# Two attention layers on one core, planned ahead: four buffers for B's divided products, new costs in the planner, a new order

## The chip, the cores and the metric

The kernel runs on one core of a Trainium2 chip. The metric is the device time of one execution in microseconds (us). Before the change the median of three runs is 492.5 us (491.84 to 493.69).

A core has engines with instruction queues of their own: PE (TensorE, matrix products into PSUM), DVE (VectorE), ACT (ScalarE), POOL (GpSimd) and SP (SyncE, which here only issues DMA transfers). Each engine works through its queue in the order in which it was written, and stops at an instruction whose semaphores have not arrived. So an instruction that is late holds up all that is queued behind it on its engine.

## The reference

The input x has 2048 tokens of 512 bfloat16 values. Two kinds of layer, A and B, are each applied twice, with the same weights both times.

```python
def _A_ref(x, wq, wk, wv, wo, beta):          # 32 heads of 16, 4 segments of 512 tokens
    ...
    for s in range(N):
        p = _softmax(qs @ ks.T * scale + mask)          # inside the segment
        a_dot = p @ vs
        a_mem = (phi(qs) @ M) / (phi(qs) @ z + 1e-6)    # memory of the earlier segments
        o = g * a_mem + (1.0 - g) * a_dot
        M = M + phi(ks).T @ vs; z = z + sum(phi(ks))
    return o @ wo

def _B_ref(x, wqkv, w_phi, wo):               # linear attention, 32 heads of 16
    q, k, v = split(x @ wqkv)
    pq, pk = q @ w_phi, k @ w_phi              # per head
    phi_q = concat(softmax(pq), softmax(-pq)); phi_k = concat(softmax(pk), softmax(-pk))
    kv = phi_k.T @ v;  z = sum(phi_k)          # over all 2048 tokens
    o = (phi_q @ kv) / (phi_q @ z + 1e-6)
    return o @ wo

x = x + _A_ref(_layernorm(x)); x = x + _B_ref(_layernorm(x))
x = x + _A_ref(_layernorm(x)); x = x + _B_ref(_layernorm(x))
```

In B, `kv` and `z` run over all tokens, so no output of B can be computed before the keys of the last tokens are done. In A, a segment needs only itself and the segments before it.

## The kernel before

The tokens lie in 16 tiles of 128; four tiles make a segment of A and a chunk of B. The program lists some 3470 operations (`Program.add`), each with the engines that may run it, a cost, what it reads and writes, and the tiles (buffers out of pools of fixed size) that it needs. Nothing of the order is written out by hand. A table `PLAN` gives each operation a priority; `sequence` turns the priorities and the dependences into one list, and `schedule` walks along it: for each engine it starts the next operation at the time when its inputs, a free buffer and the engine are there, by the costs given in `add`. The table `ON` says for some operations which of two engines takes them, and `PAIRS` says which products of queries and keys are interleaved with the next one on PE. Costs, landing times (`LANDS`, `took`, `at`) and table entries therefore decide three things: the order on every queue, the buffer each operation gets, and where PE gets filler. On the chip nobody looks at the planned times; semaphores decide.

Filler is a product of `warm` with itself into a free bank (`idle_op`, seen as L1586): where the planner sees PE idle, it puts in as many of them as fit. It keeps PE busy and computes nothing.

The parts of one run, in order: the loads and the first layer norm; A of the first layer over four segments (`a_att`, with the B keys and queries of the finished segments between); the step to the second layer, where all of B's keys must be done before the first output of B; the second A, with the first layer's B outputs of chunks 1 to 3 between; and at the end B's output for all 16 tiles.

The step around which the buffers of the change lie is `b_out`. For each tile of 128 tokens: PE multiplies `Rkv` with the exponentials of the queries (8 matmuls, names `PS<-Rkv,EQ` or `Rkv,KT`), DVE takes a reciprocal (L1488) and multiplies it on (L1489, `O<-PS,rd`), giving O, "the divided products". O is transposed, by PE (L877 `ident,O`, then a copy by ACT or DVE) or by a DMA transpose on SP's queue (L861 `OT<-O`). Then PE multiplies with `WB_o` (four matmuls), and the result is added to X. O comes from the pool `p_O`. The first PE instruction of a tile is given the buffer of O beforehand:

```python
self.pe([...Rkv products...], er + rk, [g2()], pre=[o, rd])
```

So these products wait on PE until the buffer that they will fill later is free, that is, until the transpose that read it has ended.

At the start, `setup` issues the loads on ACT's and SP's queues, ACT runs two exponentials of `beta` (L1001, L1002; the load of ACT's function table stands ahead of them), and `ln` (L1100 statistics, L1101, L1104, then L1106 on POOL, then L1115 `xn`) prepares the first tiles; their keys leave PSUM by L1181 (`KT<-PS,even`), scaled by `even` (L998).

Of the kernel before, what the change touches and what calls it, by code (L numbers as in the profile page):

```python
# [37 lines left out]
LANDS = 2.3  # L38
# [780 lines left out]
class Kernel:  # L819
# [272 lines left out]
    def ln(self, c, pris, groups=((0, 1), (2, 3)), by_pe=(), pool=None, gap=False):  # L1092

        R = self.R
# [537 lines left out]
```

## Time and profile before

| | |
|---|---|
| median of three runs | 492.5 us (491.84 to 493.69) |
| the profiled execution: its time | 492.46 us |
| its span in the profile | 490.7 us |
| instructions | 18973 |
| busy share PE, DVE, ACT, POOL | 96%, 90%, 87%, 55% |
| fillers (L1586) | 154 |

The profiled execution's own time is 1.8 us longer than its span, the part before the first and after the last instruction. A row of the time line has its start, its length, engine, source line, operation, output and inputs; a bracket at its end gives the idle time of the engine before it and what ended it. Line 799 is the helper that issues all matmuls, 855 the one that copies PSUM out, 861 and 863 the ones that issue DMA transposes and plain transfers, so there the names of the tiles tell the steps apart. A matmul's row is longer than the time until the next one starts, because matmuls overlap.

### The profile page before, as it was taken

How to read it: one execution, taken by the hardware profiler on the slowest of the kernel's cores; microseconds unless marked ns; L12 is line 12 of the kernel's file. 1: busy time of each engine (PE TensorE's matmuls, PEld its weight loads, DVE VectorE, ACT ScalarE, POOL GpSimd, SP SyncE). 2: the span in 40 equal slices, each digit the busy share in tenths (PEclk: the TensorE clock that was granted, in tenths of full speed). 3: DMA queues.
4: the chain of work that ended last, by engine and by line, in shares of the span. 5: the costliest groups of instructions: out<-in, count | busy, mean ns of one | idle time of the engine just before them, and what ended most of it. 6: DMA issues, size and time to landing. Idle time of an engine off the chain costs nothing.

```text
span 490.7 us, 18973 instructions
## 1 busy us (share of the span) xinstructions
PE 470.4 (96%) x8127; PEld 307.3 (63%) x8127; DVE 441.6 (90%) x979; ACT 425.7 (87%) x590; POOL 268.4 (55%) x536
## 2 busy tenths in 40 slices
PE   7998999999999999999999999999999999999896
PEld 6666666575657556647766666757665666575663
DVE  6998899998888999899999999999999697879785
ACT  4998999999999999783899999999999998968142
POOL 3865538656467769251256347566767364635242
PEclk9999999999999999999999999999999999999999
DMA  8965735521421221200434555352423231110234
GB/s 241 193 110 120 128 72 106 81 42 23 57 35 27 45 44 25 27 3 5 45 56 68 67 87 76 58 67 35 88 34 67 37 46 27 23 27 2 36 92 113
DMA packets 99156, 31.15 MB, mean 63 GB/s; under 512 B 90880, under 2 KB 99072, under 8 KB 99072
## 3 DMA queue, kind: packets, MB, share of 16 engines
q1 hardware_dynamic: 97824, 28.88, 35.4%
q8 instruction: 64, 1.05, 0.9%
q10 hardware_dynamic: 1248, 1.06, 0.7%
q14 instruction: 20, 0.16, 0.2%
HBM read 6.32 MB, written 2.10 MB: 17 GB/s over the span
## 4 chain that ended last, share of the span: by engine, by line
PE 47%; ACT 24%; DVE 22%; DMA 4%; issue 2%; ACTq 1%; POOL 0%; SPq 0%; DVEq 0%
PE PS L799 44%; ACT DT L1311 7%; ACT PT L1301 7%; DMA OT<-O 3%; DVE DT L1321 3%; ACT PT L1290 2%; ACT phi L1130 2%; DVE stats L1100 2%; DVE X L1364 2%; DVE PhiQ L1134 1%; PE PS L1586 1%; DVE O L1347 1%; DVE xn L1115 1%; PE PS L877 1%; DVE phi L1132 1%
## 5 line engine op out<-in xcount | busy, mean ns | idle before, releaser
L1317 POOL TENSOR_SCALAR_AFFINE_SELECT DT<-DT 64x256 bf16<-64x256 bf16 (+1 forms) x256 | 106.5, 436 | 72.2 <-ACT DT L1311 29.8
L1311 ACT ACTIVATE DT<-PS 128x1024 bf16<-128x1024 f32 x128 | 129.7, 1044 | 4.6 <-PE PS L799 3.7
L1301 ACT ACTIVATE PT<-PS 128x1024 bf16<-128x1024 f32 x128 | 128.9, 1038 | 4.7 <-PE PS L799 4.1
L1317 POOL TENSOR_SCALAR_AFFINE_SELECT DT<-PT 128x256 bf16<-128x256 bf16 x128 | 55.9, 445 | 50.0 <-PE PS L799 22.2
L799 PE MATMUL PS<-VT,DT 128*128 128x17 bf16 x1536 | 77.8, 171 | 0.8 <-POOL DT L1317 0.6
L799 PE MATMUL PS<-QT,KT 32*64 32x64 bf16 (+3 forms) x1280 | 72.6, 222 | 5.5 <-ACT DT L1311 0.9
L1398 POOL TENSOR_TENSOR Ek<-Ek,rZ 128x512 bf16<-128x512 bf16 x60 | 62.3, 1055 | 25.1 <-DVE rZ L1395 22.1
L799 PEld LDWEIGHTS PS<-VT,DT 128*128 128x128 bf16 x1536 | 70.6, 96 | 7.8 <-DVE X L1364 1.1
L799 PEld LDWEIGHTS PS<-QT,KT 32*128 32x128 bf16 (+1 forms) x1280 | 38.2, 97 | 50.5 <-ACT PT L1301 11.5
L799 PE MATMUL PS<-QT,KTo 32*64 32x64 bf16 (+3 forms) x1280 | 65.3, 216 | 0.0
L799 PEld LDWEIGHTS PS<-VT,PT 128*128 128x128 bf16 x1024 | 48.1, 96 | 8.7 <-issue 1.1
L799 PE MATMUL PS<-VT,PT 128*128 128x17 bf16 x1024 | 51.2, 171 | 0.1
L1321 DVE TENSOR_TENSOR DT<-PT,late 128x256 bf16<-128x256 bf16 x128 | 42.4, 347 | 5.5 <-PE PS L799 3.1
L1100 DVE BATCH_NORM_STATS2 stats<-X 128x6 f32<-128x512 bf16 x64 | 43.5, 685 | 1.6 <-ACT X L855 0.5
L1393 DVE TENSOR_REDUCE Zk<-Ek 128x64 f32<-128x1024 bf16 x32 | 38.5, 1203 | 4.2 <-ACT Ek L1392 4.1
L1106 POOL TENSOR_TENSOR rstd<-rstd,negh 128x2 f32<-128x2 f32 (+1 forms) x36 | 24.9, 693 | 30.5 <-DVE rstd L1104 27.1
L799 PEld LDWEIGHTS PS<-QT,KTo 32*128 32x128 bf16 (+1 forms) x1280 | 38.8, 99 | 0.1
L1392 ACT ACTIVATE Ek<-PS 128x512 bf16<-128x512 f32 x64 | 35.1, 631 | 3.1 <-PE PS L799 3.0
L799 PE MATMUL PS<-xnT,WA_q 128*128 128x128 bf16 x512 | 34.9, 219 | 0.1
L799 PE MATMUL PS<-WA_v,xnT 128*128 128x512 bf16 x128 | 34.8, 380 | 0.2
L799 PE MATMUL PS<-WA_o,OT 128*128 128x512 bf16 x128 | 32.8, 380 | 1.5 <-DMA OT<-O 0.8
L1290 ACT ACTIVATE PT<-PS 128x1024 bf16<-128x1024 f32 x32 | 33.1, 1053 | 0.4 <-PE PS L799 0.3
(146 smaller groups left out, 1009.7 us busy)
## 6 DMA issues: line engine op xcount, KB each, us to landing
EQ<-in_B_wqkv_dram SPq DMA_DIRECT2D x2, 512.0 KB, 8.2
out_dram<-X SPq DMA_DIRECT2D x8, 128.0 KB, 2.0
out_dram<-X SPq DMA_DIRECT2D x16, 64.0 KB, 2.0
X<-in_A_x_dram SPq DMA_DIRECT2D x6, 128.0 KB, 7.3
X<-in_A_x_dram SPq DMA_DIRECT2D x3, 256.0 KB, 6.6
OT<-O SPq DMA_TRANSPOSE x46, 2.5
xnT<-xn SPq DMA_TRANSPOSE x36, 2.5
WA_o<-in_A_wo_dram SPq DMA_DIRECT2D x1, 512.0 KB, 4.0
```

Source lines behind the costliest of these rows:

```text
L799: return e.matmul(o, l, r, start=st, stop=sp, tile_position=(basep(l), basep(o)))
L1100: self.dve(lambda e, t=t: e.bn_stats(self.stats[:, t, :], self.X[:, t, :]), 0.60, [R("X", t)], [R("stats", t)])
L1106: self.pool(lambda e, ve=ve, n=n: e.tensor_tensor(ve, ve, self.negh[:, 0:1].to_broadcast([128, n]), ALU.pow), 0.76, [R("rstd", t0 + i) for ...
L1130: self.act(lambda e: e.activation(shape(t2.ap), src(), ACT.Exp), 512, [res()], [t2()])
L1290: self.act(lambda e, st=st, pt=ta[y]: e.activation(pt.ap[:].rearrange("p b c -> p (b c)"), self.ps[:, st.slot[0] * 512:st.slot[0] * 512 + ...
L1301: self.act(lambda e, st=st, pt=pt: e.activation(pt.ap[:].rearrange("p b c -> p (b c)"), self.ps[:, st.slot[0] * 512:st.slot[0] * 512 + 102 ...
L1311: self.act(lambda e, st=st, dt=dt: e.activation(dt.ap[:, :, :, 64:320], self.ps[:, st.slot[0] * 512:st.slot[0] * 512 + 1024].rearrange("p ...
L1317: lambda e, c=c, src=src, base=base, p=p, block=block: e.affine_select(block(c, p), src() if src else block(c, p), [[0, 2], [0, 2], [1, 64 ...
L1321: P.add(("dve",), lambda e, early=early, block=block: e.tensor_tensor(block(320), early(), self.late[:, None, None, :].to_broadcast([128, ...
L1392: self.act(lambda e, sgn=sgn, Ek=Ek, gen=gen: e.activation(Ek.ap[:, sgn, :], self.bank(gen), ACT.Exp, scale=1.0 - 2.0 * sgn), 512, [gen()] ...
L1393: self.dve(lambda e, Ek=Ek, Zk=Zk: e.tensor_reduce(Zk.ap[:], Ek.ap[:].rearrange("p s (h j) -> p s h j", h=H), AX.X, ALU.add), 1.15, [Ek(0) ...
L1398: P.add(("dve", "pool") if late else ("pool",), lambda e, Ek=Ek, rZ=rZ, sgn=sgn: e.tensor_tensor(Ek.ap[:, sgn, :].rearrange("p (h j) -> p ...
```

## The change

The pool of O grows from two buffers to four. Five numbers of the planner change: the first landing (`LANDS`), the first key weights' transfer, the issue of a plain transfer (0.62 to 0.68), the power function on POOL (0.76 to 0.62) and the issue of four of the transposes of B's raw weights (1.28 to 1.7); and the two exponentials of `beta` may not be planned ahead of 5.1. With these the three tables were searched anew: every entry of `PLAN` may differ, `ON` moves 8 operations from DVE to ACT and 7 the other way, and `PAIRS` has 166 entries instead of 170. Nothing that is computed changes.

```diff
-LANDS = 2.3
+LANDS = 1.4
...
-    159, 165, 183, 201, 213, 243, 247, 249, 255, 267, ...
+    165, 177, 183, 195, 219, 243, 245, 249, 267, 273, ...
...
-        op = self.P.add(eng, f, 1.28 if transpose else 0.62, reads, writes, lat=1.5 if transpose else 1.3, isdma=True)
+        op = self.P.add(eng, f, (slow or 1.28) if transpose else 0.68, reads, writes, lat=1.5 if transpose else 1.3, isdma=True)
...
-        self.p_O = slots("O", 2, [128, 4, 128], BF16)
+        self.p_O = slots("O", 4, [128, 4, 128], BF16)
...
-        for k, took in (("k", (2.4, 0.4)), ("q", (1.2, 1.5)), ("v", (0.7, 1.2))):
+        for k, took in (("k", (1.9, 0.4)), ("q", (1.2, 1.5)), ("v", (0.7, 1.2))):
...
-        self.act(lambda e: e.activation(g_.ap[:, 0, :], self.beta[:], ACT.Exp, scale=-1.0), 32, [R("beta")], [g_(0)])
+        self.act(lambda e: e.activation(g_.ap[:, 0, :], self.beta[:], ACT.Exp, scale=-1.0), 32, [R("beta")], [g_(0)]).at = 5.1
...
-                self.transposed(lambda t=th[dt]: t.ap[:], lambda dt=dt, raw=raw: raw.ap[:, dt, :], [raw()], [th[dt]()], False, pre=[th[dt]])
+                self.dma(lambda t=th[dt]: t.ap[:], lambda dt=dt, raw=raw: raw.ap[:, dt, :], [raw()], [th[dt]()], transpose=True, slow=1.7 if k == "k" else 0.0)
...
-            self.pool(lambda e, ve=ve, n=n: e.tensor_tensor(ve, ve, self.negh[:, 0:1].to_broadcast([128, n]), ALU.pow), 0.76,
+            self.pool(lambda e, ve=ve, n=n: e.tensor_tensor(ve, ve, self.negh[:, 0:1].to_broadcast([128, n]), ALU.pow), 0.62,
```

Three places of the new order matter below. First, DVE at the very start. Before:

```order
10 L1100 BN_STATS stats<-X 128x6
11 L1101 BN_AGGR mv<-stats 128x2
12 L1003 TENSOR_SCALAR rd<-rd 128x32
13 L1104 TENSOR_SCALAR rstd<-mv 128x1
14 L1059 MEMSET Vt 128x32
15 L1100 BN_STATS stats<-X 128x6
16 L1101 BN_AGGR mv<-stats 128x2
17 L1115 TENSOR_SCALAR xn<-X,mv,rstd 128x512
18 L1104 TENSOR_SCALAR rstd<-mv 128x1
```

The same place after the change:

```order
9 L1115 TENSOR_SCALAR xn<-X,mv,rstd 128x512
10 L1104 TENSOR_SCALAR rstd<-mv 128x1
11 L1100 BN_STATS stats<-X 128x6
12 L1101 BN_AGGR mv<-stats 128x2
13 L1104 TENSOR_SCALAR rstd<-mv 128x1
14 L1115 TENSOR_SCALAR xn<-X,mv,rstd 128x512
15 L1003 TENSOR_SCALAR rd<-rd 128x32
16 L1004 RECIPROCAL rd<-rd 128x32
17 L1005 TENSOR_SCALAR cb<-rd 128x32
18 L1016 COPY VT<-cb 128x128 x2
19 L998 TENSOR_REDUCE even<-H 128x1
```

L1003, which reads an exponential of ACT, stood ahead of the first tile's L1104; now it stands behind the second tile's `xn`. `even` (L998), which was DVE's first instruction, now stands behind it too.

Second, SP's queue before the second segment of the first A. Before:

```order
26 L863 DMA WA_o<-in_A_wo_dram 128x4x512
27 L861 DMA_TRANSPOSE OT<-O 128x4x128
28 L863 DMA WB_v<-in_B_wqkv_dram 128x4x512
29 L861 DMA_TRANSPOSE OT<-O 128x4x128
30 L861 DMA_TRANSPOSE KT<-ktoke 128x4x128
31 L861 DMA_TRANSPOSE KTo<-ktoko 128x4x128
32 L861 DMA_TRANSPOSE KT<-ktoke 128x4x128
33 L861 DMA_TRANSPOSE xnT<-xn 128x4x128 x2
```

After:

```order
31 L863 DMA WA_o<-in_A_wo_dram 128x4x512
32 L861 DMA_TRANSPOSE OT<-O 128x4x128 x2
33 L861 DMA_TRANSPOSE KTo<-ktoko 128x4x128
34 L861 DMA_TRANSPOSE KT<-ktoke 128x4x128 x2
35 L861 DMA_TRANSPOSE xnT<-xn 128x4x128
36 L863 DMA WB_v<-in_B_wqkv_dram 128x4x512
37 L861 DMA_TRANSPOSE EQ<-xn 128x4x128
38 L861 DMA_TRANSPOSE xnT<-xn 128x4x128
39 L861 DMA_TRANSPOSE EQ<-xn 128x4x128
```

The load of `WB_v` (512 KB) has gone from between the two transposes of A's output to behind both of them, the keys' transposes and one of xn; it now stands ahead of the transposes for B's keys.

Third, PE at the start of the last `b_out`. Before:

```order
2453 L799 MATMUL PS<-Rkv,EQ 128x136 x16
2454 L1586 MATMUL PS<-warm 128x256 x11
2455 L877 MATMUL PS<-ident,O 128x128 x4
2456 L799 MATMUL PS<-Rkv,EQ 128x136 x8
2457 L1586 MATMUL PS<-warm 128x256 x2
2458 L799 MATMUL PS<-WB_o,OT 128x512 x4
2459 L799 MATMUL PS<-rhoT,sel 128x128 x16
2460 L1586 MATMUL PS<-warm 128x256 x10
2461 L799 MATMUL PS<-Rkv,EQ 128x136 x8
2462 L799 MATMUL PS<-WB_o,OT 128x512 x4
2463 L799 MATMUL PS<-Rkv,EQ 128x136 x8
```

After:

```order
2441 L799 MATMUL PS<-Rkv,EQ 128x136 x24
2442 L1586 MATMUL PS<-warm 128x256 x8
2443 L877 MATMUL PS<-ident,O 128x128 x4
2444 L799 MATMUL PS<-Rkv,EQ 128x136 x16
2445 L1586 MATMUL PS<-warm 128x256
2446 L877 MATMUL PS<-ident,O 128x128 x4
2447 L799 MATMUL PS<-Rkv,EQ 128x136 x8
2448 L799 MATMUL PS<-WB_o,OT 128x512 x4
2449 L799 MATMUL PS<-rhoT,sel 128x128 x16
2450 L799 MATMUL PS<-WB_o,OT 128x512 x4
2451 L799 MATMUL PS<-Rkv,EQ 128x136 x8
2452 L799 MATMUL PS<-WB_o,OT 128x512 x4
```

Before the first product with `WB_o` three tiles of `Rkv` products (24 matmuls) stood; now six do (48). From the first `Rkv` product to the end PE had 29 fillers and has 15; in the whole kernel 154 and 146.

More of the change, by code (lines that the diff above doesn't have):

```diff
@@ L857, in copy, with dma @@
         return self.P.add(engs, {k: emit[k] for k in engs}, {k: cost[k] for k in engs}, reads, writes, lat=0.12)
-    def dma(self, dst, src, reads, writes, eng="sp", transpose=False, took=0.3, at=0.0):
+    def dma(self, dst, src, reads, writes, eng="sp", transpose=False, took=0.3, at=0.0, slow=0.0):
         if transpose:
@@ L1000, in setup @@
         g_ = self.p_rd.tile()
-        self.act(lambda e: e.activation(g_.ap[:, 0, :], self.beta[:], ACT.Exp, scale=-1.0), 32, [R("beta")], [g_(0)])
-        self.act(lambda e: e.activation(g_.ap[:, 1, :], self.beta[:], ACT.Exp, scale=1.0), 32, [R("beta")], [g_(1)])
+        self.act(lambda e: e.activation(g_.ap[:, 0, :], self.beta[:], ACT.Exp, scale=-1.0), 32, [R("beta")], [g_(0)]).at = 5.1
+        self.act(lambda e: e.activation(g_.ap[:, 1, :], self.beta[:], ACT.Exp, scale=1.0), 32, [R("beta")], [g_(1)]).at = 5.1
         dve(lambda e: e.tensor_scalar(g_.ap[:, 0, :], g_.ap[:, 0, :], 1.0, None, op0=ALU.add), 0.15, [g_(0)], [g_(0)])
```

308 rows, old and new, of tables (ON, PAIRS, PLAN) are left out of this document.

## The prediction

> **What bounds the kernel now.** I read the engines' shares first, then the stages.
>
> ```profile
> span 490.7 us, 18973 instructions
> PE 470.4 (96%) x8127; PEld 307.3 (63%) x8127; DVE 441.6 (90%) x979; ACT 425.7 (87%) x590; POOL 268.4 (55%) x536
> ```
>
> Three engines are nearly full, but such a share is a mean over stages. Busy time by stage, from the first to the second segment, the first attention, the second attention and the last output (columns: length, then PE, PE's loads, DVE, ACT, POOL, clock, DMA share, GB/s):
>
> ```profile
> 35.00:62.00 27.00, 24.40 (x523) 16.81 (x508) 23.39 (x59) 24.33 (x30) 15.20 (x35) 1.00 0.64 120
> 62.00:204.00 142.00, 138.74 (x2648) 89.53 (x2646) 131.04 (x287) 137.79 (x183) 89.51 (x180) 1.00 0.31 50
> 245.00:455.40 210.40, 206.89 (x3692) 133.62 (x3690) 193.36 (x427) 197.49 (x272) 122.02 (x247) 1.00 0.33 51
> 455.40:490.70 35.30, 29.36 (x289) 18.99 (x285) 25.21 (x45) 10.53 (x18) 10.69 (x10) 1.00 0.38 84
> ```
>
> The attention stretches (second and third row) hold 352 of 491 us; there ACT is busy 97% and 94%: little is to be had from another order, and a worse one shows at once. The last 35 us are another matter: PE, DVE and ACT are all below their shares elsewhere. The chain that ended last has a transfer in it only in a few places; the three of O are
>
> ```profile
> 47.56 5.99 DMA OT<-O
> 460.60 4.04 DMA OT<-O
> 475.85 3.01 DMA OT<-O
> ```
>
> **The tail: four buffers.** PE's time line from the first output on, where the last two of these transfers end:
>
> ```profile
> 456.20 1.12 PE L799 MATMUL PS<-Rkv,EQ 128*128 128x136 bf16 x16 [0.18 <-DVE Rkv L1428]
> ...
> 460.86 1.27 PE L1586 MATMUL PS<-warm 128*128 128x256 bf16 x10
> 461.96 0.64 PE L799 MATMUL PS<-Rkv,EQ 128*128 128x136 bf16 x8
> 462.44 1.03 PE L799 MATMUL PS<-WB_o,OT 128*128 128x512 bf16 x4
> 464.78 0.63 PE L799 MATMUL PS<-Rkv,EQ 128*128 128x136 bf16 x8 [1.31 <-DMA OT<-O]
> 465.25 0.39 PE L877 MATMUL PS<-ident,O 128*128 128x128 bf16 x4
> ...
> 478.18 0.22 PE L799 MATMUL PS<-Rkv,KTo 128*128 128x136 bf16 x1
> 478.90 0.65 PE L799 MATMUL PS<-Rkv,EQ 128*128 128x136 bf16 x8 [0.50 <-DMA OT<-O]
> 479.39 1.03 PE L799 MATMUL PS<-WB_o,OT 128*128 128x512 bf16 x4
> 480.25 0.39 PE L877 MATMUL PS<-ident,O 128*128 128x128 bf16 x4
> ```
>
> A group of Rkv products takes 0.47 us from start to start (464.78 to 465.25), four products with WB_o 0.86 (479.39 to 480.25). With two buffers, every tile whose O is transposed by a DMA holds the Rkv products two tiles on. That costs three gaps: the fillers from 460.86 to 461.96, 1.10 us; from 462.44 + 0.86 = 463.30 to 464.78, 1.48; and from 478.18 + 0.06 (an eighth of a group) to 478.90, 0.66. Together 3.24 us. With four buffers and six tiles of Rkv products ahead of the first WB_o product, the transposed buffers are asked for about four tiles later, and a transfer has four times (0.47 + 0.86) = 5.3 us of PE work as cover against the 4.04 above. Of the other fillers of the tail, at 1.10 / 10 = 0.11 us each, four more go (29 become 15, ten are already counted): 0.44 us.
>
> What is late next is DVE, which must make each O:
>
> ```profile
> 458.24 0.35 DVE L1488 RECIPROCAL rd<-PS 128x32 f32<-128x32 f32 x1
> 459.29 0.36 DVE L1488 RECIPROCAL rd<-PS 128x32 f32<-128x32 f32 x1
> ...
> 462.64 0.36 DVE L1488 RECIPROCAL rd<-PS 128x32 f32<-128x32 f32 x1 [0.27 <-PE PS L799]
> 465.45 0.36 DVE L1488 RECIPROCAL rd<-PS 128x32 f32<-128x32 f32 x1 [1.73 <-PE PS L799]
> 478.44 0.36 DVE L1488 RECIPROCAL rd<-PS 128x32 f32<-128x32 f32 x1 [0.75 <-PE PS L799]
> ...
> 487.09 0.69 DVE L1364 TENSOR_TENSOR X<-X,PS 128x512 bf16<-128x512 bf16 x1 [1.64 <-PE PS L799]
> ```
>
> A tile costs DVE 1.05 us (458.24 to 459.29) against PE's 0.47 + 0.86 and, for most, a transpose. At the three gaps DVE idles 0.27 + 1.73 + 0.75 = 2.75 us. So much it can catch up; the rest of the 3.7 us would find O not yet made. I take 2.8 for the tail. The bounds: 3.7, and 1.3, the idle that is seen at 464.78 alone, if all else turns into waits for O.
>
> **35 to 62 us: WB_v moved.** PE's wait for the transpose that the chain above has at 47.56, the fillers behind it, and EQ's transposes (SP) with their first use (PE):
>
> ```profile
> 53.60 1.04 PE L799 MATMUL PS<-WA_o,OT 128*128 128x512 bf16 x4 [0.84 <-DMA OT<-O]
> 56.66 1.04 PE L1586 MATMUL PS<-warm 128*128 128x256 bf16 x8
> 58.11 2.50 SPq L861 DMA_TRANSPOSE EQ<-xn  x2
> 63.33 1.03 PE L799 MATMUL PS<-WB_v,EQ 128*128 128x512 bf16 x4
> ```
>
> and the landing times there (44 to 58 us):
>
> ```profile
> WB_v<-in_B_wqkv_dram SPq DMA_DIRECT2D x1, 512.0 KB, 4.7
> xnT<-xn SPq DMA_TRANSPOSE x3, 2.5
> OT<-O SPq DMA_TRANSPOSE x2, 4.9
> ```
>
> Transposes behind the load land after 4.9 us instead of 2.5, 2.4 late. Once they stand ahead of it, the 0.84 goes, and of the eight fillers before the second segment's strips four remain (the new PE queue has three and one there): 0.4. I take 1.0. Now the transposes of EQ and xnT stand behind the load. In the old queue the second of EQ's started at 58.11 + 1.25 and landed 2.5 later, at 61.9, for a use at 63.3; so up to 2.4 - 1.4 = 1.0 us of such a delay may show. Bounds: a gain of 1.3, a loss of 1.0. The Trainium skill, "DMA: Bandwidth & Descriptors", section "Where 436 GB/s comes from", gives about 358 GB/s for HBM to SBUF, by which 512 KB hold the engines for an estimated 1.5 us. By that the 0.84 would only go in part, and the term would be about 0.6; the landing rows above say 2.4, and I keep to them.
>
> **The start.** Before:
>
> ```profile
> 3.83 1.28 ACT L1002 ACT_TABLE_LOAD   x1 [3.83 <-issue]
> 5.50 0.18 DVE L1003 TENSOR_SCALAR rd<-rd 128x32 f32<-128x32 f32 x1 [1.09 <-ACT rd L1001]
> 6.49 0.38 DVE L1115 TENSOR_SCALAR xn<-X,mv,rstd 128x512 bf16<-128x512 bf16 x1
> 7.61 0.41 DVE L1115 TENSOR_SCALAR xn<-X,mv,rstd 128x512 bf16<-128x512 bf16 x1 [0.68 <-POOL rstd L1106]
> 8.24 0.94 DVE L1016 COPY VT<-cb 128x128 bf16<-128x128 bf16 x2
> 9.41 0.69 ACT L1181 ACTIVATE KT<-PS,even 128x512 bf16<-128x512 f32 x1 [0.30 <-PE PS L799]
> 15.14 1.03 PE L799 MATMUL PS<-WA_v,xnT 128*128 128x512 bf16 x4
> ```
>
> DVE waited 1.09 us for an exponential that the first tile doesn't need. With L1003 moved the first xn comes about 1 us earlier; the second, behind one more statistic (0.7 us) but without POOL's 0.68 wait, some 0.5. The keys' products follow by as much. But L1181 now also needs `even`, which stands behind the second xn (7.1 + 0.4), three small steps (0.7 together) and L1016's 0.94: 9.2 us, so of the 0.5 only 0.2 reaches ACT. The table load goes ahead of the issue of half of WA_v, which shifts it by 1.28 + 0.2; its first use is at 15.1 us, and it stays covered. I take a gain of 0.2, bounds 0.6 each way (the whole shift, or `even` as late as that).
>
> **Other edits.** ON's net moves give ACT one more copy of 0.6 us and DVE one less: 0.2 lost, bounds 0 to 0.6, since ACT is the fullest engine between 62 and 204. Four strips fewer are interleaved. The nearest row for eight short matmuls by themselves is a group of Rkv products, 0.47 us, so the bound is 1.9 where PE is late; with ACT at 97% I take 0. The rest of PLAN reorders about a fifth of PE's instructions, most between 245 and 290 and between 370 and 420. No row prices that. I take 0 and bounds of 2.5 each way: ACT's idle in the second and third row is 4.2 + 12.9 us, and a fifth of it, gained or added, is 3.4, and a part of that always lies beside other waits. The power's and the transfers' costs are planner entries and act only through the order.
>
> **Sum:** -2.8 - 1.0 - 0.2 + 0.2 = -3.8. From the profiled execution's 492.46 us (span 490.7 and 1.8 around it) that gives 488.7; the median of the runs, 492.5, is the same execution to 0.01%.
>
> **Rivals.**
> 1. *The tail is DVE's* (O isn't ready when its buffer is). PE waits then for O where it waited for a buffer; the four buffers do nothing for the end. For it: DVE's 1.05 us a tile and X and EQ besides. Against: its idle of 2.75 us at just these gaps. Then only the second of the visible waits goes, 0.50: 488.7 + 2.3 = 491.0.
> 2. *WB_v stalls the second segment's B keys*: 1.0 is lost instead of gained, 490.7.
> 3. *The attention stretches starve ACT* and the kernel gets slower. Mechanism: in the reordered fifth the strips of queries and keys come behind longer blocks on PE, and ACT waits for PS. In the worst 12.27 us slice of the old attention (404.9 to 417.2) that was already so:
>
> ```profile
> 404.91:417.18 12.27, 11.75 (x233) 8.17 (x234) 9.50 (x23) 10.87 (x14) 6.03 (x16) 1.00 0.13 27
> ```
>
> ACT idles 1.40 us there, against 17.1 / 28.7 slices = 0.60 in the mean. If nine slices more went like this one, 9 x 0.80 = 7.2 us would be added: 488.7 + 7.2 = 495.9. From 3.8 us of added ACT idle on the gain is gone, from 6.3 the kernel is slower by 0.5%. For it: a new search follows the planner's costs, not the chip's. Against: the old order came out of the same planner with nearly the same costs, and ACT is 97% busy under it.
>
> **How the numbers follow.** The runs span 0.4%, so about 0.5% (2.46 us) is what a measurement can tell from no change. My forecast, below 490.0, has 0.60; rival 1 has 0.19 and rival 2 0.08, both within 0.5%; rival 3 0.13. So faster 0.60, same 0.27, slower 0.13. The range: at the low end the tail's 3.7 and most of the 2.5 of the reorder, 488.7 - 0.9 - 1.8 = 486.0; at the high end it holds rivals 1 and 2 and the loss of 2.5 on top of rival 1, 491 + 2.5 = 493.5, and leaves out most of rival 3.
>
> **What would show it.** In the new profile the tail from the first Rkv product (456.2 before) to the last X (487.8) should be 28.8 us instead of 31.6, with no idle of 1 us on PE before an Rkv product. Waits of PE or PEld for `O` (L1489) of more than 2 us in sum would show rival 1. OT<-O near 50 us should land in 2.5 to 4 us; EQ near 60 later than 4.6 with PE waiting for it is rival 2. ACT's idle between 62 and 204 should stay near 4.2 us; above 8 it is rival 3. I am wrong if the tail shrinks by less than 1.3 or if the stretches move by more than 2.5 us either way.

## The result and the profile after

The changed kernel takes 486.1 us (median of four executions, 485.4 to 488.8), the kernel before in the same comparison 492.2 (490.9 to 493.7): ratio 0.989, interval 0.984 to 0.993. The forecast was 488.7. The gain is 6.0 us by the medians; a second comparison (fourth experiment) gives 7.0. The profiled execution of the changed kernel, though, is its slowest, 488.78: 3.7 us under the profiled one of before, which is the forecast's 3.8 almost to the tenth. That agreement is an accident, as the experiments show. The median of 486.1 itself lies just inside the forecast's range, whose low end is 486.0.

First the head of its page:

```profile
span 487.0 us, 18857 instructions
...
PE 458.4 (94%) x8027; PEld 306.6 (63%) x8119; DVE 436.0 (90%) x978; ACT 426.1 (87%) x591; POOL 266.6 (55%) x536
```

The same four stages as in the prediction (length, then PE, PE's loads, DVE, ACT, POOL, clock, DMA share, GB/s):

```profile
35.00:62.00 27.00, 24.76 (x516) 17.62 (x519) 24.42 (x61) 25.42 (x32) 14.87 (x34) 1.00 0.62 115
62.00:204.00 142.00, 136.52 (x2653) 90.44 (x2683) 130.68 (x289) 138.68 (x184) 88.40 (x181) 1.00 0.32 52
245.00:454.30 209.30, 201.45 (x3645) 133.42 (x3688) 190.44 (x427) 198.75 (x274) 122.36 (x249) 1.00 0.31 51
454.30:487.00 32.70, 26.98 (x272) 17.82 (x272) 24.12 (x46) 10.43 (x18) 10.73 (x10) 1.00 0.36 91
```

ACT idles 142 - 138.68 = 3.3 us in the first attention (4.2 before) and 209.3 - 198.75 = 10.6 in the second (12.9 before). Of the tail, the rows of PE's time line that have a wait, and DVE's last instruction:

```profile
455.12 1.59 PE L799 MATMUL PS<-Rkv,EQ 128*128 128x136 bf16 x24 [0.18 <-DVE Rkv L1428]
...
460.71 0.40 PE L799 MATMUL PS<-rhoT,sel 32*128 32x128 bf16 x16 [0.25 <-DVE O L1489]
...
462.26 1.04 PE L799 MATMUL PS<-WB_o,OT 128*128 128x512 bf16 x4 [1.14 <-DMA OT<-O]
```

```profile
483.18 0.69 DVE L1364 TENSOR_TENSOR X<-X,PS 128x512 bf16<-128x512 bf16 x1 [1.25 <-PE PS L799]
```

From the first Rkv product to the end of the last X: 483.18 + 0.69 - 455.12 = 28.75 us, 31.58 before. Three groups of Rkv products go off at once, and none waits for a buffer any more; what is left is a product with WB_o that waits 1.14 for its own O.

To compare many profiles I use three sections, bounded by two DVE rows: the division of Rkv (L1428) is done in each layer at the step where B's keys are complete, in pieces that DVE and POOL share; DVE's first piece belongs to the first layer, its last to the second. The answer for that line gives its first and its last start, to 0.1 us. Of before, of the changed kernel, and of its second profile (fourth experiment):

```profile
L1428 DVE TENSOR_TENSOR Rkv<-KV,H x3: 435/576/709, 223.1 to 455.4; 128x408 bf16<-128x408 f32 x2, 128x272 bf16<-128x272 f32 x1
```

```profile
L1428 DVE TENSOR_TENSOR Rkv<-KV,H x3: 435/578/707, 223.6 to 454.4; 128x408 bf16<-128x408 f32 x2, 128x272 bf16<-128x272 f32 x1
```

```profile
L1428 DVE TENSOR_TENSOR Rkv<-KV,H x3: 436/577/708, 220.3 to 451.1; 128x408 bf16<-128x408 f32 x2, 128x272 bf16<-128x272 f32 x1
```

All profiles by these rows, in us; "tail" here runs from the second L1428 to the end of the last X. The ratio is that of the executions to those of the kernel before in the same comparison.

| kernel | ratio (95%) | to the first L1428 | second layer | tail |
|---|---|---|---|---|
| before | | 223.1 | 232.3 | 32.4 |
| changed | 0.989 (0.984 to 0.993) | 223.6 | 230.8 | 29.5 |
| e1 four buffers alone | 0.998 (0.995 to 1.001) | 226.8 | 233.2 | 30.2 |
| e2 buffers, order of the tail | 0.997 (0.994 to 0.999) | 223.9 | 233.2 | 29.3 |
| e3 all but the tail, two buffers | 0.994 (0.992 to 0.997) | 223.3 | 231.7 | 31.4 |
| e4 changed, once more | 0.986 (0.983 to 0.989) | 220.3 | 230.8 | 29.4 |
| e5 WB_v's load later | 0.999 (0.996 to 1.001) | 223.0 | 232.3 | 31.9 |
| e6 planner's costs alone | 1.001 (0.999 to 1.003) | 224.1 | 232.2 | 31.9 |
| e7 changed, start of before | 0.989 (0.986 to 0.991) | 221.6 | 230.8 | 29.7 |
| e8 first layer's order from 35 us | 0.997 (0.995 to 0.999) | 221.9 | 232.3 | 31.8 |
| e9 changed, two transposes swapped | 0.988 (0.986 to 0.990) | 222.3 | 230.8 | 29.4 |
| e10 the same, X load earlier | 0.989 (0.987 to 0.992) | 224.2 | 230.8 | 29.7 |
| e11 changed, three buffers | 0.993 (0.990 to 0.995) | 221.7 | 230.8 | 32.2 |
| e12 as e1, fewer fillers | 1.001 (0.998 to 1.003) | 223.6 | 233.2 | 29.8 |

The second layer is the same to 0.1 us in all profiles with the same order and buffers (before, e5, e8 and, with the same order, e6; e1, e2 and e12; six of the changed order). The first section is not, and there a single profile misleads: the order of before reaches its end at 223.1 (before) and at 224.1 (e6). In e1, e10 and e11 it also holds time at half the PE clock (last section).

### The profile page after: what moved, and what is told of

The parts are those of the page before. It is cut to its first block, busy times and chain, and to the rows that moved or that the text cites. A ratio compares the mean times of both kernels' runs of the same rounds, so it can differ in the third digit from the quotient of the medians.

```text
span 487.0 us, 18857 instructions
## 1 busy us (share of the span) xinstructions
PE 458.4 (94%) x8027; PEld 306.6 (63%) x8119; DVE 436.0 (90%) x978; ACT 426.1 (87%) x591; POOL 266.6 (55%) x536
## 4 chain that ended last, share of the span: by engine, by line
PE 41%; DVE 26%; ACT 24%; DMA 4%; issue 2%; SPq 1%; POOL 1%; DVEq 0%
PE PS L799 39%; ACT PT L1301 7%; ACT DT L1311 7%; DVE stats L1100 3%; DMA X<-in_A_x_dram 3%; ACT PT L1290 3%; DVE Zk L1393 2%; DVE X L1364 2%; DVE DT L1321 2%; ACT Ek L1392 2%; ACT phi L1130 1%; ACT EQ L1443 1%; PE PS L1586 1%; DVE O L1347 1%; PE PS L877 1%
## 5 line engine op out<-in xcount | busy, mean ns | idle before, releaser
L1317 POOL TENSOR_SCALAR_AFFINE_SELECT DT<-PT 128x256 bf16<-128x256 bf16 x128 | 54.3, 433 | 44.5 <-PE PS L799 24.2
L1321 DVE TENSOR_TENSOR DT<-PT,late 128x256 bf16<-128x256 bf16 x128 | 39.7, 323 | 3.7 <-PE PS L799 3.4
L799 PE MATMUL PS<-WA_o,OT 128*128 128x512 bf16 x116 | 30.2, 379 | 3.3 <-DVE r L1346 1.1
L799 PEld LDWEIGHTS PS<-xnT,WA_q 128*128 128x128 bf16 x512 | 29.9, 98 | 4.3 <-issue 0.6
```

The source lines that it names most:

```text
L799: return e.matmul(o, l, r, start=st, stop=sp, tile_position=(basep(l), basep(o)))
L1317: lambda e, c=c, src=src, base=base, p=p, block=block: e.affine_select(block(c, p), src() if src else block(c, p), [[0, 2], [0, 2], [1, 64 ...
L1321: P.add(("dve",), lambda e, early=early, block=block: e.tensor_tensor(block(320), early(), self.late[:, None, None, :].to_broadcast([128, ...
```

## The experiments

**One: buffers, tail, the rest.** The two orders agree on which operations stand ahead of the 3332nd (the first of the tail) and ahead of the 1651st (the end of the first layer), so pieces of one can be followed by pieces of the other.

```diff
 e1: tables and costs of before
-        self.p_O = slots("O", 2, [128, 4, 128], BF16)
+        self.p_O = slots("O", 4, [128, 4, 128], BF16)
 e2: the same line, and
-PLAN, ON, PAIRS: operations 3332 to 3474 as in before
+PLAN, ON, PAIRS: operations 3332 to 3474 as in the changed kernel
 e3: changed kernel with
-        self.p_O = slots("O", 4, [128, 4, 128], BF16)
+        self.p_O = slots("O", 2, [128, 4, 128], BF16)
-PLAN, ON, PAIRS: operations 3332 to 3474 as in the changed kernel
+PLAN, ON, PAIRS: operations 3332 to 3474 as in before
 e4: changed kernel, no edit
```

> The kernel before with four O buffers in place of two; its tables of order, its engine choices and its planner's costs stay. If the buffers by themselves take away the waits of the tail (the forecast's ground for -2.8), the tail from the first Rkv product to the end of the last X goes from 31.6 to about 28.8 us and the time falls by 2 to 3. If the buffers only pay with an order of the instructions that uses them, the Rkv products stand as late in PE's row as before and the tail stays above 30.5, the time within 1 of the kernel before. Before the tail nothing changes by either.

> The kernel before with four O buffers and the changed kernel's order for the last 143 operations alone (the tail); everything ahead of them stands as before, the planner's costs too. By the forecast the tail is worth 2.8: tail 28.8 us, time 489.4 where the kernel before has 492.2. If the tail is worth less than the 2.83 seen between the two profiles, and the gain lies in the stretch ahead of it, the time falls by under 1.5.

> The changed kernel with two O buffers and the order of before in the last 143 operations (the tail); all ahead of them, and the planner's costs, stand as in the changed kernel. Tail 31.6 us by either theory. If the two profiled executions tell the truth, the work ahead of the tail gains 1.1 and the time falls by about 1. If the medians do (6.0 in all, of which 2.8 are the tail's), it falls by about 3.

> The changed kernel once more, unaltered, in the same comparison as the parts. Its gain should be the sum of the two parts (tail only, all but the tail): about -4 if the profiled execution of the first time is typical, about -6 if its 80th VT product at 43.9 us (41.2 before) was that execution's own late start; in that case the 80th VT product stands at 41 to 42 us in this profile.

Measured: medians 492.1 (e1), 491.5 (e2), 489.8 (e3), 486.7 (e4) against 493.6. The buffers by themselves shorten the tail to 30.2 us, most of the way, and the tail's new order takes it on to 29.3. But both kernels with four buffers and before's order also lose 0.9 us in the second layer (233.2 for 232.3), so that e2 gains less than its tail, 1.7 us by its ratio and not the 2.8 of its expectation, and e1 cannot be told from no change (0.995 to 1.001). All but the tail gains 2.8 us by its ratio, nearer to what the medians said (about 3) than to what the profiles did (1). And the second profile of the changed kernel reaches the first L1428 at 220.3, 3.3 us earlier than the first profile, with not an instruction changed. By the ratios e4 gains 7.0 us, the two parts together 1.7 + 2.8 = 4.5, so they do not add up as its expectation had it; 0.9 + 0.9 of the difference is the second layer, where e2 has 233.2 and e3 231.7 against 232.3 and 230.8. The rest is within what the first section varies by.

**Two: which piece ahead of the tail.**

```diff
 e5: kernel before; SP's queue ahead of the second segment
-WA_o load, OT<-O, WB_v load, OT<-O, KT, KTo, KT, xnT, xnT
+WA_o load, OT<-O, OT<-O, KT, KTo, KT, xnT, WB_v load, xnT
 e6: tables and two buffers of before, and
-LANDS = 2.3
+LANDS = 1.4
 ... and the other costs of the change
 e7: changed kernel with
-PLAN, ON, PAIRS: operations 1 to 272 as in the changed kernel
+PLAN, ON, PAIRS: operations 1 to 272 as in before
 e8: kernel before with
-PLAN, ON, PAIRS: operations 273 to 1650 as in before
+PLAN, ON, PAIRS: operations 273 to 1650 as in the changed kernel
```

> The kernel before with one issue moved: the load of WB_v stands in SP's queue behind the four transposes that follow it in before (OT<-O, KT, xnT, KTo) and one xnT, as in the changed kernel; nothing else moves. The forecast put -0.6 on this move, within -1.0 for its stage. If the load is what makes the stage of 51 to 62 us late, the seventh reciprocal L1346 (62.7 us in the profile of before, 60.8 in the changed kernel's second profile) comes 1 to 2 us earlier and the time falls by as much. If the stage gains by the order of PE, DVE and ACT instead, nothing moves: within 0.5 of the kernel before.

> The kernel before with the changed planner's costs alone (first transfers 1.4 instead of 2.3, issue 0.68, ScalarE's first exponentials not before 5.1, and the rest); order, engine choices and two O buffers as before. The queues hold the same instructions in the same order, with other counts of fillers. Forecast: nothing, within 0.5. If the costs matter by themselves (through fillers and banks), over 1 either way.

> The changed kernel with the first 272 operations (to about 35 us) in the order of before; the rest, four O buffers and the costs as in the changed kernel. If the late start of two of the three profiles of the new order (PE waits 1.9 us for an OT<-EQ transpose near 30 us, DVE 0.7 to 1.1 for an X load queued behind two transposes) comes from the new order of SP's first issues, the first three reciprocals L1346 stand at 24.1, 32.5 and 37.9 us as in all profiles of before, no PE wait for OT<-EQ is over 0.5 us, and the time is that of the changed kernel without its late executions: 485 to 486 where the changed kernel's median is 486.1 to 486.7, or 7 to 8 under the kernel before. If the start varies from execution to execution whatever the order, the profile shows the wait again and the median does not move. If the new start is itself worth the forecast's 0.2, the time is 0.2 longer.

> The kernel before with the changed order only from the 273rd operation (about 35 us) to the end of the first layer (about 221 us); start, second layer, tail, costs and two O buffers as before. By the changed kernel's second profile this piece gains 2.8 (first division of Rkv L1428 at 220.3 us, 223.1 before): the time falls by 2.5 to 3. By the forecast (1.0 in 35 to 62 us, nothing behind) it falls by 1, with the WB_v load's move accounting for 0.6 of it. If the gain of the new order lies in the second layer, under 0.5.

Measured: 492.5 (e5), 493.3 (e6), 487.6 (e7), 491.4 (e8) against 492.9. The costs do nothing that can be told from no change. The first layer's order from 35 us on gains 1.2 (223.1 to 221.9) in the profile and 1.5 by its ratio (0.6 to 2.4), less than the 2.5 to 3 that I read from the second profile. WB_v's load alone is not settled. PE's time line of e5 has no wait for OT<-O any more; PE stands at this product with WA_o at 52.62 instead of 53.60, and stays 0.85 ahead until 59.8. Then it stalls on something that the profile does not name, and the lead is gone:

```profile
52.62 1.04 PE L799 MATMUL PS<-WA_o,OT 128*128 128x512 bf16 x4
...
60.83 0.22 PE L799 MATMUL PS<-QT,KT 32*64 32x64 bf16 x3 [0.63 <-issue]
```

The profiles of before, of the changed kernel (both), of e7 and e8 have no such stall there. By its executions e5 gains 0.7 us, interval -0.3 to 1.8. The seventh reciprocal L1346, the sign that I had set for this experiment, stands at 62.45, 0.2 earlier than in before and not 1 to 2.

e7 compares the two starts: its first L1428 stands at 221.6, between the changed kernel's 220.3 and its 223.6. So the new start gains 1.3 us in one execution and loses 2.0 in another. In the median it cannot be told from the old one: e7 takes 487.6 and not the 485 to 486 that I expected, with the changed kernel's ratio. The 1.3 is not there at the end of the start either: the fifth reciprocal L1346 stands at 49.01 in e7 and at 48.88 in the changed kernel's second profile, the seventh at 61.97 and 60.84. Why it comes only there is open.

For the late execution the rows point to SP's queue. B's raw weights are transposed there (`OT<-EQ`) for eight folding products on PE (`PS<-O,OT`, four for the keys, four for the queries). SP's queue in the changed kernel's first profile:

```profile
12.57 2.47 SPq L861 DMA_TRANSPOSE OT<-EQ  x1
15.09 3.61 SPq L861 DMA_TRANSPOSE PhiK<-phi  x1
18.75 0.62 SPq L863 DMA_DIRECT2D X<-in_A_x_dram  x1
19.41 6.01 SPq L861 DMA_TRANSPOSE OT<-EQ  x4
...
26.78 1.27 SPq L861 DMA_TRANSPOSE OT<-EQ  x1
```

The first two folding products on PE, and DVE's wait for X:

```profile
27.36 0.40 PE L799 MATMUL PS<-O,OT 128*128 128x128 bf16 x4 [0.40 <-DVE O L1347]
...
30.85 0.40 PE L799 MATMUL PS<-O,OT 128*128 128x128 bf16 x4 [1.90 <-DMA OT<-EQ]
...
24.45 0.69 DVE L1100 BATCH_NORM_STATS2 stats<-X 128x6 f32<-128x512 bf16 x1 [1.09 <-DMA X<-in_A_x_dram]
```

The same places of its second profile:

```profile
14.78 2.20 SPq L861 DMA_TRANSPOSE PhiK<-phi  x1
17.02 0.62 SPq L863 DMA_DIRECT2D X<-in_A_x_dram  x1
...
25.28 1.27 SPq L861 DMA_TRANSPOSE OT<-EQ  x1
```

```profile
26.41 0.39 PE L799 MATMUL PS<-O,OT 128*128 128x128 bf16 x4
...
27.83 0.39 PE L799 MATMUL PS<-O,OT 128*128 128x128 bf16 x4
```

The new order puts one X load behind two transposes (in before all X loads are ahead of them), and the transpose that the second folding product reads sixth among the OT<-EQ (in before it is second). The issue of `PhiK<-phi` took 3.61 us in one execution and 2.20 in the other; so the X load went out at 18.75 or at 17.02, and in the first case DVE waits 1.09 us for it and PE 1.90 for a transpose that was issued at 26.78. In the second case neither waits. Two more profiles of the same order fit: with 2.91 us for that transpose and X at 17.83 (e3) the waits are 0.74 and 1.98, with 2.07 and 16.61 (e11, below) there are none. None of the eight profiles with the start of before has either wait.

**Three: mending the start, three buffers, and where e1 lost.**

```diff
 e9: changed kernel; SP's queue, OT<-EQ by the folding product that reads it
-4th of keys, PhiK, X load, 1st, 3rd, 1st and 3rd of queries, PhiK, 2nd of keys
+2nd of keys, PhiK, X load, 1st, 3rd, 1st and 3rd of queries, PhiK, 4th of keys
 e10: as e9, and
-2nd of keys, PhiK, X load, 1st
+X load, 2nd of keys, PhiK, 1st
 e11: changed kernel with
-        self.p_O = slots("O", 4, [128, 4, 128], BF16)
+        self.p_O = slots("O", 3, [128, 4, 128], BF16)
 e12: e1 with
-                n = gap(op, t)
+                n = 0 if i in (1808, 1898) else gap(op, t)
```

> The changed kernel with two DMA transposes OT<-EQ of the folded weights changing places in SP's queue: the one that PE's second folding product reads goes first, and the one that its last reads goes sixth (the changed order has them the other way round; in before the second product's stands ahead of four others). If that place is what makes the changed kernel's start late in some executions (transpose issued 25.3 to 26.8 us, PE's second folding product at 27.8 or, with a wait of 1.9, at 30.6 to 30.9), no PE wait for OT<-EQ near 30 us is left, the first division of Rkv L1428 stands at 220.3 to 221.5 us whatever the execution, and the time's spread shrinks to under 2.5 us with a median of 485 to 486.5. The wait of DVE for a late X load (0.7 to 1.1 near 24 us) stays in some executions and costs up to 1. If the late X load is the cause and the transpose only follows it, the wait of 1.9 moves to another instruction and L1428 still stands at 223 in some profiles.

> As the swap of the two transposes, and the X load that the changed order queues behind two transposes stands ahead of them again, as in before. Both waits should be gone: DVE none over 0.4 for X near 24 us, L1428 at 220 to 221 us, time 485 to 486, within 1 of the swap alone; if only the X load matters, this one is faster than the swap alone by 0.5 or more in the median, and by up to 3 in its slowest executions.

> The changed kernel with three O buffers instead of four, same order. If three do (two tiles in flight and one being written), tail and time stay as in the changed kernel (tail 28.7, time within 0.5). If the changed order needs the fourth, PE stands in the tail before an Rkv product or a third tile's O until the first O is read: tail 1 to 3.5 us longer, with the wait in PE's or DVE's row at O L1489.

> The kernel before with four O buffers (as in the first experiment), and without two batches of fillers (4 and 1 products of warm) that the planner put into the second layer once there were four buffers. Those profiles with before's order and four buffers took 233.2 us from the first to the second division of Rkv L1428, all with two buffers 232.2 to 232.3. If the fillers at these two places are the cause, 232.3 again, and the time is 0.9 under the first experiment's. If it is the buffers themselves (another transpose landing elsewhere), 233.2 stays. The tail stays at 30.2 from L1428 to the end of the last X (31.3 to 32.4 with two buffers, 29.3 to 29.7 with the changed order).

Measured: 486.9 (e9; 486.3 to 487.7), 487.4 (e10), 488.0 (e11), 492.5 (e12) against 492.5. The swap does what it should to PE's second product, but X came later still in this execution, and the first product waits on it by way of DVE. PE and DVE of e9:

```profile
27.77 0.40 PE L799 MATMUL PS<-O,OT 128*128 128x128 bf16 x4 [1.09 <-DVE O L1347]
...
29.20 0.39 PE L799 MATMUL PS<-O,OT 128*128 128x128 bf16 x4
...
24.86 1.29 DVE L1100 BATCH_NORM_STATS2 stats<-X 128x6 f32<-128x512 bf16 x2 [1.88 <-DMA X<-in_A_x_dram]
```

So the late X costs time by itself too, and L1428 came at 222.3, later than the limit of 221.5 in my expectation; the spread did shrink to 1.5 us, over six executions. With the X load earlier (e10) DVE's wait for X falls to 0.57 us (at 22.64; I expected none over 0.4), and something else is late: the transpose `PhiK<-phi` moved from 15.18 in e9 to 17.70, and ACT waits for the buffer that it reads, then PE for ACT. SP, ACT and PE of e10:

```profile
13.61 4.04 SPq L861 DMA_TRANSPOSE OT<-EQ  x1
17.70 2.12 SPq L861 DMA_TRANSPOSE PhiK<-phi  x1
...
26.15 0.60 ACT L1130 ACTIVATE phi<-PS 128x512 bf16<-128x512 f32 x1 [3.31 <-DMA PhiK<-phi]
...
28.21 0.26 PE L799 MATMUL PS<-QT,KT 32*128 32x192 bf16 x2 [2.90 <-ACT DT L1311]
```

Neither of the two can be told from the changed kernel in the executions (0.988 and 0.989), so none beats it. That SP's queue makes the start late is thus read from these waits and from e7, where the whole order of the start is taken back and they are gone; that one place in it is to blame is not shown.

Three buffers keep the second layer's 230.8, but the tail is 32.2 us. PE and DVE of e11, where the fourth tile's Rkv products want the first tile's buffer:

```profile
456.27 2.78 PE L1586 MATMUL PS<-warm 128*128 128x256 bf16 x24
...
459.73 0.65 PE L799 MATMUL PS<-Rkv,EQ 128*128 128x136 bf16 x8 [0.68 <-DMA OT<-O]
```

```profile
460.41 0.36 DVE L1488 RECIPROCAL rd<-PS 128x32 f32<-128x32 f32 x1 [2.60 <-PE PS L799]
```

24 fillers and 0.68 us stand where the changed kernel has products, and DVE starves for 2.60. The changed tail with two buffers was not tried: in that order the queues would wait for one another.

e12 refutes my reading of e1. I had taken five fillers that the planner adds once there are four buffers for the cause of the 0.9 us in the second layer. Without them it is 233.2 again. Where the first batch stood PE now waits; of e12, and of before at the same place:

```profile
254.46 0.26 PE L799 MATMUL PS<-QT,KT 32*128 32x192 bf16 x4 [0.59 <-ACT PT L1290]
```

```profile
253.27 0.26 PE L799 MATMUL PS<-QT,KT 32*128 32x192 bf16 x4
```

In the program with four buffers this product waits for one instruction more of ACT (a count of 311, not 310), since the planner gave its PSUM banks to the strip just ahead of it. That is, another number of buffers moved the planned times, these moved the banks, and the fillers only filled the wait. The banks themselves were not changed by an experiment, so this cause is read from the waits and not shown by itself.

## Why the prediction came out as it did

**The tail (-2.8).** The mechanism held: the waits for a buffer went, no Rkv product is preceded by 1 us of idle, and the tail that was to be 28.8 us by the prediction's own measure is 28.75. Over all profiles the size was a little smaller: five tails with before's order and two buffers take 31.4 to 32.4 us (mean 31.9), six with the changed order and four take 29.3 to 29.7 (mean 29.5), so -2.4. Of it 1.9 come by the buffers alone (e1 and e12, mean 30.0) and 0.5 by the order. The gain stayed below 3.7, as the cap by DVE had it: DVE has no wait over 0.15 us from 454.4 to 463.4 in the changed tail. That DVE is what holds the tail there is not shown by an experiment, and PE's wait of 1.14 is for a transfer. Rival 1, in which the tail stays as long, is refuted: PE's longest wait for O at L1489 is 0.25, and PE and its weight loads together wait 1.7 us for O in this tail (0.2 + 1.1 + 0.4), under the 2 that were to show it.

**35 to 62 us (-1.0).** The order from there to the end of the first layer gave 1.2 in e8, but only 0.6 of it by the seventh reciprocal L1346, near the end of this stage. Before and e8:

```profile
62.67 0.25 DVE L1346 RECIPROCAL r<-PS 128x16 f32<-128x16 f32 x1
```

```profile
62.07 0.25 DVE L1346 RECIPROCAL r<-PS 128x16 f32<-128x16 f32 x1
```

So by this profile the term was 0.4 too large, and 0.6 came behind 62 us, where the prediction had nothing. The step behind the term, the move of WB_v's load, isn't settled: the wait of 0.84 goes, the forecast's ground, but the profile of e5 loses the lead again. (With before's order this wait is itself 0.84 to 1.76 us long: before, e6, e2, e1.) (The expectation of e5 names 0.6 for this move; that was the term by the estimate from the page, the forecast's own was 1.0.) One sign was wrong: both transposes of O near 50 us were to land in 2.5 to 4 us and took 5.4; they now stand behind WA_o's load, which I had not counted. The landing times of the changed kernel's first profile, 44 to 58 us:

```profile
WA_o<-in_A_wo_dram SPq DMA_DIRECT2D x1, 512.0 KB, 4.4
...
OT<-O SPq DMA_TRANSPOSE x2, 5.4
KT<-ktoke SPq DMA_TRANSPOSE x2, 2.5
```

Behind a load of 512 KB a transpose is 5.4 - 2.5 = 2.9 us late here. The prediction also gave an estimate of 1.5 us by the Trainium skill, "DMA: Bandwidth & Descriptors", section "Where 436 GB/s comes from"; the rows of both kernels say more.

Rival 2 did not happen: e8 has WB_v's load at its new place in SP's queue, and gains.

**The start (-0.2, within 0.6).** This term was mis-sized. I followed DVE and ACT through the first 10 us and did not follow SP's queue from 12 to 27 us, where the new order moves an X load and two transposes. Measured against e7's 221.6, by one profile each: -1.3 when they are in time (220.3), and +2.0 and +1.7 when not (223.6, and 223.3 in e3). The -1.3 comes between 49 and 62 us, behind the start, its cause is open, and the medians do not settle it.

**The rest of PLAN (0, within 2.5).** It gained 1.5 in the second layer, 232.3 to 230.8, in every profile. 0.9 of that is had only with more than two buffers (e3: 231.7), while before's order loses 0.9 by them. Which part of the order does it is not shown. Rival 3 is refuted: ACT's idle between 62 and 204 us is 3.3 us, and 142 - 137.75 = 4.25 in the second profile, where 8 would have shown it. (The prediction calls ACT the fullest engine there; by its own row PE is, with 138.74 against 137.79.) The costs by themselves act only through the order, as forecast.

**The sum.** -1.3 - 1.2 - 1.5 - 2.4 = -6.4 us for an execution whose start is in time; the two comparisons say 6.0 and 7.0. The terms of the first layer are good to about 1 us, by what profiles of one order differ. The forecast of -3.8 missed 2.6 of this, all of it ahead of the tail: 1.5 by the rest of PLAN, 1.1 by the start, 0.2 by the first layer from 35 us on, and 0.2 that it put down as a loss by ON's moves and that no section shows, less the 0.4 by which the tail fell short. The median still lies in the range because its low end allowed 1.8 for a gain of the rest of PLAN. The profiled execution's -3.7 matched it only since its late start gave 3.3 back.

## What to carry to other kernels

Cut a searched order at places where both versions have done the same operations, and join the pieces: that tells which stretch gains, where one number for the whole cannot. More buffers and the order that uses them belong together: alone the buffers gave the tail 1.9 us and took 0.9 elsewhere, and three under the order made for four gave the tail nothing. Before you believe the difference of two profiles, take a second profile of the same kernel and look at which stretch of it repeats to 0.1 us and which does not.

## What the runs showed of the hardware

**The issue of a DMA transpose does not always take the same time.** On SP most take 1.27 us (26.78 above), but the first ones took 2.1 to 4.0 in the rows from 12 to 20 us above (2.47, 3.61, 2.20, 4.04, 2.12). The same one takes 3.61 in one execution of a kernel and 2.20 in another, and all that is queued behind it on SP varies with it. That the loads of the start are the reason is not shown: the kernel before issues its first transpose right behind five loads of X in 1.29 us, and in the changed kernel's first profile two together take 3.42 with no load issued between 190 and 202 us. Before, and the changed kernel:

```profile
14.28 1.29 SPq L861 DMA_TRANSPOSE PhiK<-phi  x1
```

```profile
198.41 3.42 SPq L861 DMA_TRANSPOSE xnT<-xn  x2
```

**PE's clock falls to half for 3.4 us at a time.** Windows of 1 us in e10, behind the wait of 2.90 us shown above; the third number from the right is the granted clock:

```profile
28.00:29.00 1.00, 0.79 (x15) 0.74 (x16) 0.52 (x1) 1.00 (x3) 0.72 (x2) 0.92 0.38 76
29.00:30.00 1.00, 1.00 (x10) 0.75 (x8) 0.00 (x0) 0.99 (x2) 0.86 (x4) 0.50 0.42 83
...
31.00:32.00 1.00, 1.00 (x10) 0.59 (x10) 0.97 (x5) 0.41 (x2) 1.00 (x3) 0.50 0.43 90
32.00:33.00 1.00, 1.00 (x15) 0.95 (x13) 1.00 (x2) 1.00 (x2) 0.92 (x4) 0.87 1.12 57
```

(0.08 + 0.5 + 0.5 + 0.5 + 0.13) / 0.5 = 3.4 us at half speed (30 to 31 us shows 0.50 as well). e1 has two such windows (below 0.17 x 10 and 0.10 x 17, each 1.7 us lost), the second behind a wait of 1.76 us, and therefore the latest first section in the table:

```profile
55.68 1.04 PE L799 MATMUL PS<-WA_o,OT 128*128 128x512 bf16 x4 [1.76 <-DMA OT<-O]
```

```profile
35.00:45.00 10.00, 8.69 (x175) 6.58 (x162) 7.45 (x20) 7.21 (x10) 4.63 (x12) 0.83 0.47 83
45.00:62.00 17.00, 14.99 (x268) 9.53 (x265) 13.37 (x34) 13.81 (x17) 8.44 (x20) 0.90 0.76 126
```

The length of the wait ahead does not tell when. e11 has such a window behind waits of no more than 0.54 us, and e12 keeps the full clock behind one of 1.75, as the changed kernel's first profile does behind its 1.90. The wait and the clock behind it, e11 and e12:

```profile
153.01 0.22 PE L799 MATMUL PS<-QT,KT 32*64 32x64 bf16 x4 [0.54 <-POOL DT L1317]
```

```profile
154.30:157.70 3.40, 3.40 (x64) 3.27 (x62) 2.65 (x7) 2.25 (x4) 2.27 (x6) 0.51 0.56 67
```

```profile
39.49 0.87 PE L799 MATMUL PS<-VT,PhiK 128*128 128x136 bf16 x12 [1.75 <-ACT WB_q L855]
```

```profile
41.00:44.40 3.40, 3.40 (x95) 3.03 (x94) 3.33 (x10) 2.76 (x4) 1.28 (x4) 1.00 1.05 82
```

A mean clock of 0.996 over some 490 us is one window, 0.992 two: of the executions of before beside e1, 13 with 0.999 or more have a median of 492.8 us, 13 with 0.995 to 0.997 have 494.3, three with 0.992 or 0.993 have 496.2. Beside e5 the three medians are 492.7 (16), 494.7 (8) and 494.1 (3), so the price of a second window is not clear. The Trainium skill, "TensorE: Matmul & The Clock Gate", section "What's actually happening", has the half clock and the window of 3.4 us, and the trace agrees with both. By the same section of the Trainium skill the half clock comes after an idle window of that length. Here PE was busy for 0.59 us (e10), 2.09 and 1.64 (e1) and 2.74 (e11) of the 3.4 us ahead of it. What decides is open.
